# A decayed linear attention feeding a three-way maxout layer: a new order of all engines' instructions

## The chip, the cores and the metric

The kernel runs on one core of one Trainium2 chip. The metric is the device time of one execution in microseconds (us), lower is better; three executions of the kernel before gave 149.94, 150.0 and 150.5 us.

## The reference

Two parts, one after the other. The first is a gated linear attention over 4 batches, 8 heads, 768 tokens and 48 channels a head; the second is a layer over all 3072 tokens with three weight matrices, of whose products the largest is kept.

```
for t in range(S):                                   # S = 768
    state = alpha[:, :, t, :, None] * state + einsum('bhd,bhe->bhde', k[:, :, t], v[:, :, t])
    y[:, :, t] = einsum('bhd,bhde->bhe', q[:, :, t], state)
x = y.transpose(0, 2, 1, 3).reshape(3072, 384)
h = maximum(maximum(x @ w1, x @ w2), x @ w3)         # 384 -> 768
out = h @ w_out                                      # 768 -> 384
```

All inputs and the output are float32 in the chip's main memory.

## The kernel before, in words

**Steps.** The recurrence is done in chunks. The tokens are cut into 12 steps s, each of 256 tokens of one batch: batch s % 4, chunk of tokens s // 4. Within a step the work splits into two units x = 0, 1 of 128 tokens. Inside a unit the products of all pairs of tokens are formed at once (scores, mask, values); between units the state, 48 x 48 a head, is carried on. The layer then runs over the 256 tokens of the step: nine products into PSUM (three blocks jg of 256 columns of the hidden layer, three weights g) and, last, the output product for each unit.

**Pieces.** All work is cut into pieces, and a text called ORDER lists them; `emit` walks through that list and issues each piece's instructions on its engine. A piece is written as a letter, an index, sometimes an engine's letter, and the step: `q1v@3` is piece q with index 1 of step 3 on VectorE. The engine letters are v (VectorE, DVE in the profile), p (GpSimd, POOL) and a (ScalarE, ACT). The engine letter on a load chooses the queue that issues it: SyncE's (SP) without a letter, ScalarE's with a. Without another choice each engine runs its pieces strictly in the order in which the list has them, and waits at a piece until what that piece reads is there and what it writes is free.

The letters, with the function and the line that the profile shows:

| letter | function | engine | what it does |
|---|---|---|---|
| l0, l1, l2, l3 | load_step (L96) | SP or ACT queue | loads alpha (tile ra), k (rk), q (rq), v (rv) of a step, 384 KB each |
| K, W | load_weight (L107, L110), cast_weight | queue; POOL or ACT | one of 12 pieces of 384 KB of the weights into tile ws, then its cast into wcat or wo |
| H | warm (L435) | PE | so many 512-column products of zeros, whose result nobody reads |
| m, N, r | pair_decay, logs, inverse (L183, L187, L192, L194) | DVE/POOL, ACT | product of two tokens' decays, logarithms, the inverse of a decay |
| c | sums (L207, L209) | PE | running sums of the logarithms (tile lps) |
| f, e, g | decay_out, decay_in, totals (L221, L217, L225) | ACT | exponentials of those sums (tiles ac, ic, ge) |
| u, w | near_k, near_q (L198, L202) | DVE/POOL | k and q of every first token times its neighbour's decay (tiles ka, qa) |
| k, q | scale_k, scale_q (L231) | DVE/POOL | k and q times the exponentials (tile qk) |
| V, v | values, unit_values (L155, L157; copies L149, L151) | any | v in 16 bits (tile vt), then in the layout of a unit (tile vu) |
| T, t | turn, keep_turned (L265; copies) | PE; DVE/ACT | transposes of qk through PSUM, and the copy out (tile qkT); steps 0 to 4 |
| D | turn_by_dma (L273) | SP queue | the same by a transposing DMA; steps 5 to 11 |
| A, a | scores, masked (L286, L293) | PE, DVE | products of all pairs (two PSUM tiles aps), masked on the way out (tile lat) |
| Y, x | attend (L306), keep_x | PE; DVE/ACT | the attention's output (tile yps), copied out as the layer's input xT |
| S, s, M, z, y | update (L357), add_state (L367), gates (L344), decay_state (L372), spread_state | PE, DVE, POOL, ACT | the state: product, sum, gate factors, decay, copy in 16 bits (tile st) |
| G, h | gate (L388), maxed (L405; copies) | PE; ACT, DVE | a product of the layer (tile gps; index 3 jg + g), and its maximum with the one before |
| O, o | project (L421), store (L155, L157; DMA L430) | PE; ACT/DVE, SP | the output product (tile ops), scaled out (tile ob) and stored |

A copy or a multiplication through a helper is seen in the profile at the helper's line: L149 and L151 for copies, L155 and L157 for multiplications by a column.

**What ties the pieces.** Loads go into rings of four tiles for each of alpha, k, q and v, so the load of step s waits until the pieces of step s - 4 have read their tile. PSUM has eight banks, taken in turn by every product on PE; scores take two at a time. Weights come in as float32 into eight staging tiles. Output tiles, transposed tiles and the others have two to eight buffers. The order of the list is written out; nothing in the kernel computes it.

Of the kernel before, what the change touches and what calls it, by code (L numbers as in the profile page):

```python
# [23 lines left out]
def kernel(  # L24
# [422 lines left out]
    def emit(order):  # L447
# [14 lines left out]
        g0@3 K5@0 K3@0 e0@3 h1v@0 V0a@2 S0@2 s0a@2 h0v@1 q0p@2 h1v@1 T0@2 t0a@2 t1v@2 W5p@0 G5@1
        G5@0 W3a@0 z0p@2 y0a@2 s1v@2 l0@4 v1p@2 h2v@0 K4@0 h2v@1 r0@4 A1@2 A0@2 a0@2 G3@1 h3a@1
        Y3@2 m0p@4 W4p@0 l3a@3 a3@2 G3@0 N0@4 a1@2 v0p@2 l1@3 r0@3 G4@1 c0@4 g0@4 a2@2 Y2@2
        x1v@2 h3a@0 Y0@2 x0a@2 u0p@3 h4v@1 l0@5 G4@0 h5v@1 M1p@0 z1p@0 y1a@0 G0@2 h0a@2 G5@2
        r1@3 G1@2 K6@0 W6a@0 G3@2 h4v@0 h5v@0 h1v@2 G2@2 l2@3 k0p@3 w0v@3 q0v@3 K7@0 G6@2 V0a@3
        h3a@2 l2@4 l1@4 r1@4 m0p@5 M0p@3 h2v@2 G4@2 h4v@2 k1p@3 S0@3 s0v@3 N0@5 G6@1 h6a@2 h5v@2
        W7p@0 r0@5 G7@2 h7v@2 T0@3 q1p@3 T1@3 G7@1 z0p@3 K8@0 e0@4 w0p@4 f0@4 l3@4 s1v@3 v0a@3
        t1v@3 t0a@3 k1v@4 G6@0 h6a@1 q1p@4 h7v@1 l2@6 u0p@4 c0@5 A0@3 a0@3 A1@3 T1@4 q0p@4 a2@3
        W8a@0 G8@2 a3@3 h8v@2 G8@0 g0@5 h6a@0 a1@3 f0@5 G8@1 k0p@4 T0@4 e0@5 h8v@1 G7@0 v1p@3  # L470
        Y0@3 Y2@3 t1a@4 V0a@4 t0a@4 h7v@0 y0p@3 Y3@3 x0a@3 x1a@3 K11@0 l1@5 K9a@0 v1p@4 S0@4
        W11a@0 A0@4 s0v@4 K10a@0 a1@4 A1@4 a3@4 M0p@4 z0p@4 s1v@4 u0p@5 G0@3 l0@6 a0@4 G7@3
        l1a@6 a2@4 v0v@4 y0a@4 m0p@6 r0@6 G3@3 h3a@3 G1@3 G6@3 Y0@4 r1@5 l3a@5 h0v@3 Y3@4 h8v@0
        Y2@4 x1v@4 N0@6 Y1@4 x0a@4 W9a@0 l2@5 G8@3 M1v@1 c0@6 e0@6 f0@6 G0@4 h1v@3 k0v@5 q1v@5
        G3@4 w0v@5 q0v@5 M0p@5 W10a@0 g0@6 u0v@6 r1@6 G1@4 l0@7 m0v@7 G2@4 k1p@5 D1@5 h0a@4
        z1p@1 k0p@6 O0@1 h1v@4 w0v@6 D0@5 q0p@6 D0@6 k1p@6 q1p@6 O1@1 N0@7 l0@8 h6a@3 l3@6 h2v@4
        l2@7 l1a@7 o1a@1 h7v@3 D1@6 h3v@4 o0a@1 V0a@5 O0@2 o0a@2 O1@2 y1p@1 G7@4 h8v@3 S0@5 A0@5
        s0v@5 o1a@2 a0@5 a1@5 A1@5 a3@5 a2@5 v1a@5 z0p@5 G4@4 v0p@5 r0@7 u0p@7 y0a@5 G2@3 G6@4
        s1v@5 M1p@2 z1p@2 y1p@2 h4v@4 c0@7 Y3@5 Y1@5 Y2@5 m0p@8 Y0@5 e0@7 k0p@7 h2v@3 h6v@4
        h7v@4 G5@4 x0a@5 f0@7 G4@3 x1a@5 l1@8 N0@8 G8@4 V0a@6 h8v@4 r1@7 w0p@7 G0@5 h0a@5 h5v@4  # L480
        h4v@3 k1v@7 G3@5 h3a@5 G1@5 h1v@5 c0@8 e0@8 g0@7 f0@8 M1p@3 G5@3 h5v@3 G4@5 Y1@6 A1@6
        g0@8 M0p@8 r0@8 h4v@5 A0@6 a1@6 l3@7 S0@6 s0v@6 M0p@6 q0v@7 D0@7 q1p@7 z0p@6 D1@7 G6@5
        a3@6 h6a@5 G7@5 l0@9 l2@8 G5@5 G2@5 z1p@3 O0@0 s1v@6 v1a@6 a2@6 y0a@6 y1p@3 v0a@6 Y3@6
        a0@6 Y2@6 Y0@6 O1@0 x1v@6 o0a@0 l0@10 r1@8 l3a@8 x0v@6 G4@6 G3@6 V0a@7 v1a@7 G0@6 h5v@5
        M1v@4 z1p@4 G8@5 h2v@5 h3a@6 h7v@5 h4v@6 S0@7 h0a@6 v0p@7 l3@11 o1a@0 h8v@5 y1a@4 A0@7
        a1@7 s0v@7 u0p@8 A1@7 a2@7 m0p@9 a3@7 M0p@7 z0p@7 y0p@7 k0p@8 Y1@7 a0@7 r0@9 l1a@9 G2@6
        G1@6 h1v@6 q1p@8 G6@6 h6v@6 s1v@7 G5@6 Y0@7 Y2@7 N0@9 l2@9 m0v@10 w0v@8 q0p@8 D0@8 Y3@7
        k1v@8 D1@8 x0a@7 x1a@7 l3@9 G8@6 G7@6 r1@9 G6@7 h6a@7 G0@7 V0v@8 c0@9 e0@9 O1@3 g0@9
        M1p@5 u0v@9 k0v@9 O0@3 f0@9 w0p@9 G4@7 q1p@9 k1p@9 D1@9 q0p@9 D0@9 o1a@3 o0a@3 V0a@11
        h2v@6 h5v@6 h7v@6 h8v@6 G8@7 G7@7 h7v@7 h0a@7 S0@8 N0@10 s0v@8 O0@5 o0a@5 A0@8 a0@8 A1@8  # L490
        a2@8 l0@11 Y1@8 G3@7 v1a@8 h3a@7 l1a@10 O1@5 c0@10 a3@8 z0p@8 y0p@8 Y3@8 o1a@5 a1@8 Y2@8
        e0@10 h8v@7 g0@10 v0p@8 Y0@8 G1@7 x0a@8 f0@10 V0a@9 v0p@9 x1v@8 G1@8 h4v@7 l2@10 M1v@6
        z1v@6 z1v@5 y1a@5 l3@10 G0@8 h1v@7 M0p@9 h0a@8 S0@9 A1@9 A0@9 s0v@9 z0p@9 y0p@9 G6@8
        l1@11 G2@8 a0@9 v1p@9 G2@7 G5@7 h6a@8 r0@10 r1@10 M0p@10 u0p@10 Y3@9 a3@9 a1@9 a2@9
        m0v@11 l2a@11 q1p@10 k1v@10 D1@10 Y0@9 Y1@9 x0a@9 Y2@9 G7@8 h2v@7 h1v@8 x1a@9 r0@11 G4@8
        G8@8 G6@9 G3@9 w0p@10 N0@11 c0@11 f0@11 h5v@7 e0@11 h6v@9 V0v@10 q0v@10 k0p@10 D0@10
        O0@4 O1@4 g0@11 v0a@10 h7v@8 h2v@8 G4@9 h8v@8 G5@8 O1@7 r1@11 v1p@10 S0@10 h3a@9 h4v@9
        o0a@4 o1a@4 q1p@11 k1v@11 o1a@7 M1p@7 D1@11 s0v@10 A0@10 a0@10 A1@10 a3@10 u0p@11 k0p@11
        G7@9 z0p@10 y0a@10 y1p@6 G8@9 G3@8 h3a@8 O0@7 a1@10 w0v@11 a2@10 h7v@9 h8v@9 Y3@10 Y1@10
        Y0@10 Y2@10 G1@9 G0@9 x1v@10 x0a@10 G4@10 z1p@7 q0p@11 D0@11 h4v@8 h0a@9 h5v@8 h1v@9  # L500
        G2@9 G3@10 o0a@7 v1p@11 h2v@9 S0@11 s0v@11 A0@11 A1@11 a0@11 a3@11 h3a@10 G6@10 G0@10
# [42 lines left out]
```

## Time and profile before

| what | value |
|---|---|
| time, median of 3 runs (lowest to highest) | 150.0 us (149.94 to 150.5) |
| span of the profiled execution, first to last instruction | 147.1 us |
| time of the profiled execution itself | not on the page; the median is 2.9 us above its span |
| PE busy | 137.7 us, 94% of the span |
| DVE, ACT, POOL busy | 120.5, 100.7, 89.7 us |
| DMA | 32.43 MB, 220 GB/s on average |
| TensorE clock granted | 1.000 |

Busy times of a line of the profile are the union of its instructions; an instruction's duration is a mean over its group. An "idle before" time says how long the engine stood before the instruction, and the name behind the arrow is what ended the wait. A row of the timeline has the start, the time taken, the engine (with a q behind it where only the engine's sequencer works, as in issuing a DMA), the line, the operation and the tiles, out before in.

### The profile page before, as it was taken

The numbers are of one execution on the slowest core, as the hardware profiler recorded it, in microseconds if no ns is written. First come the engines' busy times: TensorE is split into PE (matmuls) and PEld (weight loads), VectorE is DVE, ScalarE is ACT, GpSimd is POOL, SyncE is SP. The second block draws the span as 40 slices with busy tenths as digits, with TensorE's granted clock in tenths as the row PEclk, the third lists the DMA queues.
The fourth block names the chain that finished last, engine by engine and source line by source line (L and its number), as shares of the span: only waits on it lengthen the run. The fifth ranks groups of instructions, "written<-read, shape, count | busy, mean of one in ns | idle before, by whom it ended". The sixth has DMA issues, their size and how long they took to land.

```text
span 147.1 us, 5524 instructions
## 1 busy us (share of the span) xinstructions
PE 137.7 (94%) x2301; PEld 105.4 (72%) x2301; DVE 120.5 (82%) x224; ACT 100.7 (68%) x207; POOL 89.7 (61%) x147
## 2 busy tenths in 40 slices
...
GB/s 114 321 325 341 326 312 282 322 288 334 328 298 241 286 225 155 202 289 187 303 156 325 327 218 155 237 269 276 288 117 222 91 113 0 4 75 37 53 241 134
DMA packets 73032, 32.43 MB, mean 220 GB/s; under 512 B 65456, under 2 KB 73008, under 8 KB 73008
## 3 DMA queue, kind: packets, MB, share of 16 engines
...
q10 hardware_dynamic: 9152, 4.03, 10.5%
...
## 4 chain that ended last, share of the span: by engine, by line
PE 38%; DMA 18%; POOL 16%; ACT 9%; SPq 8%; issue 4%; DVE 4%; POOLq 0%; DVEq 0%; ACTq 0%
PE gps L388 21%; DMA rv<-in_v_dram 11%; PE ops L421 10%; SPq L96 7%; POOL qk L231 6%; DMA ws<-in_moe_w_dram 5%; PE yps L306 3%; DMA qkT<-qk 3%; POOL kept L372 2%; POOL ka L198 2%; PE aps L286 2%; POOL st L151 2%; ACT vu L149 1%; POOL wcat L151 1%; POOL vu L151 1%
## 5 line engine op out<-in xcount | busy, mean ns | idle before, releaser
L388 PE MATMUL gps<-xT,wcat 128*128 128x256 f16 x648 | 76.5, 273 | 1.5 <-DVE hT L405 0.6
L388 PEld LDWEIGHTS <-wcat 128*128 128x128 f16 x648 | 61.2, 98 | 11.7 <-issue 1.1
L293 DVE TENSOR_TENSOR lat<-aps,cp 128x512 f16<-128x512 f32 x48 | 30.3, 681 | 0.5 <-PE aps L286 0.3
L405 DVE TENSOR_TENSOR h<-gps,h 128x512 f16<-128x512 f32 x36 | 24.6, 684 | 2.4 <-PE gps L388 1.2
L405 DVE TENSOR_TENSOR hT<-gps,h 128x512 f16<-128x512 f32 x36 | 24.1, 684 | 1.9 <-PE ops L421 1.3
L421 PE MATMUL ops<-wo,hT 128*128 128x384 f16 (+1 forms) x150 | 25.2, 320 | 0.2 <-ACT h L149 0.2
L149 ACT CAST h<-gps 128x512 f16<-128x512 f32 x28 | 16.2, 583 | 9.0 <-PE gps L388 7.0
L421 PEld LDWEIGHTS <-hT 128*128 128x128 f16 x150 | 14.1, 98 | 8.2 <-issue 0.4
L155 ACT ACTIVATE ob<-ops,c 128x384 f32<-128x384 f32 (+1 forms) x23 | 12.2, 567 | 11.4 <-PE ops L421 11.3
L372 POOL TENSOR_TENSOR kept<-full,gm 128x192 f32<-128x192 f32 x18 | 10.3, 573 | 10.5 <-DVE gm L344 5.0
L151 POOL COPY vu<-vt 64x384 f16<-64x384 f16 x24 | 12.2, 509 | 4.7 <-ACT vt L155 2.8
L149 ACT CAST xT<-yps 128x384 f16<-128x384 f32 x17 | 7.8, 490 | 7.3 <-PE yps L306 7.3
L231 POOL TENSOR_TENSOR qk<-ka,ic 128x384 f16<-128x384 f32 x10 | 10.5, 1054 | 3.6 <-ACT h L149 2.6
L149 ACT COPY vu<-vt 64x384 f16<-64x384 f16 x22 | 11.2, 510 | 0.7 <-DVE vt L157 0.3
L435 PE MATMUL wps<-wo 128*128 128x512 f16 x35 | 9.7, 425 | 1.2 <-DVE wo L511 1.2
L155 ACT ACTIVATE vt<-rv,c 128x768 f16<-128x768 f32 x10 | 9.4, 941 | 1.6 <-DMA rv<-in_v_dram 1.5
L231 POOL TENSOR_TENSOR qk<-rq,ac 128x384 f16<-128x384 f32 x8 | 8.3, 1036 | 1.7 <-DMA rq<-in_q_dram 1.7
L286 PE MATMUL aps<-qkT 48*64 48x128 f16 x384 | 7.7, 219 | 1.3 <-DVE qkT L151 0.8
L198 POOL TENSOR_TENSOR ka<-rk,ra 128x384 f32<-128x384 f32 x8 | 8.4, 1044 | 0.2
L306 PE MATMUL yps<-lat,vu 128*32 128x128 f16 x384 | 8.0, 220 | 0.3 <-DVE lat L293 0.2
L231 POOL TENSOR_TENSOR qk<-rk,ic 128x384 f16<-128x384 f32 x6 | 6.2, 1040 | 3.1 <-DMA rk<-in_k_dram 3.0
L192 ACT ACTIVATE ra<-ra 128x384 f32<-128x384 f32 x12 | 6.3, 524 | 2.5 <-DMA ra<-in_alpha_dram 2.4
...
## 6 DMA issues: line engine op xcount, KB each, us to landing
...
```

Source lines behind the costliest of these rows:

```text
L149: nc.scalar.copy(out=dst, in_=src)
L151: engines[eng].tensor_copy(out=dst, in_=src)
L155: nc.scalar.mul(dst, src, col)
L198: engines[eng or "p"].tensor_mul(near_of[s, "k"], raw("k", s, 0), raw("a", s, 1))
L231: engines[eng or "p"].tensor_mul(dst.rearrange("p a b c -> p (a b) c")[:, :, :D], near_of.pop((s, n)) if r == 0 else raw(n, s, r), dec_of[ ...
L286: nc.tensor.matmul(aps[i][r * J:(r + 1) * J, a * U + x, :], qkT[rows, r, 1, p, cols], qkT[rows, :, 0, p, cols], start=True, stop=True)
L293: nc.vector.tensor_mul(lat_of[s, u][:, i], aps_of[s, u][i], pmask.unsqueeze(1).broadcast_to([P, HP, P]))
L306: nc.tensor.matmul(y_of[s, x][C * m:C * (m + 1), f, :], lhs, rhs, start=(s, x, m) not in begun, stop=last[x] and n == len(todo) - 1)
L372: engines[eng or "p"].tensor_mul(kept, full_of.pop((s, x)), gm_of.pop((s, x)).unsqueeze(2).broadcast_to([P, HP, D]))
L388: nc.tensor.matmul(gps[:, j, :], wcat[:, f, g, jj * P:(jj + 1) * P], xT[:, f].rearrange("p u t -> p (u t)"), start=(f == 0), stop=(f == NF ...
L405: nc.vector.tensor_max(h, gps, h_of[s, i - 1])
L421: nc.tensor.matmul(ops_of[s, o], hT_of[s][:, jj, u * P:(u + 1) * P], wo16[:, jj, cols], start=(jj == 0), stop=(jj == NJ - 1))
```

## The change

The list ORDER is replaced by another. Both have the same 818 pieces: no piece, tile or buffer is added or taken away. What differs is the order, on every engine, and the engine or queue of some pieces:

| pieces | engine or queue before | after |
|---|---|---|
| loads l | SP 40, ACT 8 | SP 29, ACT 19 |
| weight loads K | SP 10, ACT 2 | SP 7, ACT 5 |
| weight casts W | ACT 8, POOL 4 | ACT 5, POOL 7 |
| values V | ACT 10, DVE 2 | ACT 7, DVE 2, POOL 3 |
| unit_values v | ACT 11, POOL 12, DVE 1 | ACT 15, POOL 9 |
| scale_q q | POOL 14, DVE 10 | POOL 10, DVE 14 |
| scale_k k | POOL 16, DVE 8 | POOL 17, DVE 7 |
| near_q w | DVE 7, POOL 5 | DVE 4, POOL 8 |
| near_k u, pair_decay m | DVE 4 and 6, POOL 8 and 6 | DVE 5 and 7, POOL 7 and 5 |
| gates M | POOL 17, DVE 3 | POOL 13, DVE 7 |
| decay_state z | POOL 18, DVE 2 | POOL 13, DVE 7 |
| spread_state y | POOL 10, ACT 9, DVE 1 | POOL 9, ACT 11 |
| keep_x x | ACT 17, DVE 7 | ACT 14, DVE 10 |
| store's scaling o | ACT 23, DVE 2 | ACT 17, DVE 8 |
| maxed h, add_state s | one h from ACT to DVE | one s from DVE to ACT |

The start and the end of both lists:

```diff
     ORDER = """
-        l0@0 r0@0 H12@0 H4@0 H1@0 m0p@0 N0@0 c0@0 r1@0 l0@1 m0v@1 l2@0 H1@0 r0@1 f0@0 g0@0 H4@0
-        w0p@0 l1@0 u0v@0 q0v@0 N0@1 c0@1 e0@0 l3@0 V0a@0 r1@1 e0@1 f0@1 l0@2 k1v@0 q1v@0 M0p@0
-        l2@1 k0p@0 l1@1 k1p@1 m0v@2 w0v@1 H10@0 g0@1 N0@2 S0@0 s0a@0 T1@0 t1a@0 c0@2 q1v@1 T0@0
-        z0p@0 f0@2 e0@2 g0@2 q0v@1 H1@0 l3@1 V0a@1 t0v@0 A1@0 A0@0 T1@1 H2@0 u0v@1 a2@0 k0p@1
-        S0@1 T0@1 K1@0 v1a@0 v0p@0 a1@0 a3@0 a0@0 Y0@0 W1a@0 Y2@0 t1v@1 y0p@0 s0a@1 M0p@1 z0p@1
-        Y3@0 l0@3 v1a@1 t0v@1 m0v@3 A1@1 A0@1 x0a@0 x1a@0 G1@0 K2@0 W2p@0 G2@0 l1@2 a2@1 v0a@1
-        y0p@1 Y3@1 k1p@2 u0p@2 a1@1 N0@3 c0@3 a3@1 a0@1 Y0@1 r0@2 r1@2 K0@0 W0a@0 x0v@1 Y2@1
-        x1a@1 l2@2 s1v@0 s1v@1 f0@3 k0p@2 w0v@2 G0@0 l3@2 M0p@2 G1@1 G0@1 G2@1 h0a@0 q1v@2 T1@2
...
-        G6@11 h6a@11 G4@11 O1@9 h4v@11 O0@9 o0v@9 h2v@11 O0@6 O1@10 o1a@10 O1@6 h7v@11 h5v@11
-        O4@11 h8v@11 o1a@9 O6@11 o0a@6 o1a@6 o2a@11 O2@11 O3@11 o0a@11 O5@11 o1a@11 O0@10 o0a@10
+        H12@0 H10@0 l0@0 m0v@0 r0@0 H4@0 l0@1 N0@0 m0v@1 r1@0 c0@0 H1@0 r0@1 l2@0 f0@0 g0@0 q1v@0 w0v@0
+        N0@1 r1@1 l1a@1 H1@0 H2@0 e0@0 l1@0 l0a@2 c0@1 l3a@1 g0@1 M0p@0 u0v@0 M0v@1 k1v@0 k0v@0 T1@0 l1a@2
+        q0v@0 T0@0 f0@1 t1v@0 l3@0 l2@1 q1v@1 V0a@0 e0@1 v1a@0 w0p@1 u0v@1 S0@0 H4@0 K1a@0 k1v@1 t0a@0
+        m0v@2 K0a@0 A1@0 s0a@0 z0p@0 A0@0 r0@2 r1@2 k0p@1 l2a@2 a2@0 a1@0 T1@1 N0@2 V0a@1 H1@0 K2@0 v0a@1
+        c0@2 S0@1 l3a@2 a0@0 q0v@1 s0a@1 e0@2 v0p@0 y0p@0 W1a@0 T0@1 z0p@1 y0p@1 a3@0 t1v@1 Y0@0 Y2@0
+        t0v@1 Y3@0 x0v@0 K4@0 A1@1 x1a@0 A0@1 a2@1 a1@1 G1@0 W0a@0 l0@3 G0@0 g0@2 a0@1 a3@1 W2p@0 G2@0
+        f0@2 v1a@1 Y3@1 h0a@0 q1v@2 w0v@2 Y0@1 u0v@2 x0a@1 M0p@2 Y2@1 x1a@1 k1p@2 T1@2 h1v@0 k0v@2 G1@1
+        q0p@2 G0@1 T0@2 t1a@2 W4a@0 h2v@0 h0a@1 G4@1 s1v@1 s1v@0 V0p@2 t0a@2 S0@2 A1@2 h1v@1 v1a@2 v0p@2
+        m0v@3 a3@2 A0@2 G4@0 N0@3 a0@2 s0a@2 K3@0 W3p@0 G2@1 z0p@2 l0@5 m0p@5 K5@0 W5p@0 c0@3 K6a@0 r0@3
...
+        Y1@9 Y2@9 Y0@9 G4@8 x0a@9 O1@7 x1v@9 h4v@8 D0@11 h2v@8 h5v@8 G0@9 h0a@9 G1@9 S0@10 V0v@11 A0@10
+        o1a@7 A1@10 v1a@11 a0@10 a3@10 h1v@9 O0@8 s0v@10 a1@10 G6@9 h6a@9 a2@10 O1@8 S0@11 A0@11 s0v@11
+        o0a@8 A1@11 G7@9 M0p@10 z0p@10 a1@11 a2@11 y0p@10 y1a@6 G3@9 a0@11 v0p@11 z0v@11 G4@9 G2@9 G5@9
...
+        h4v@11 o0a@9 h5v@11 O2@11 h8v@11 O3@11 o0v@10 o1a@10 o0v@11 O4@11 O5@11 O6@11 o1a@11 o2v@11
     """
```

SP's queue up to l3@4 has, in the old order: l0@0 l0@1 l2@0 l1@0 l3@0 l0@2 l2@1 l1@1 l3@1 K1 l0@3 K2 l1@2 K0 l2@2 l3@2 K5 K3 l0@4 K4 l1@3 l0@5 K6 l2@3 K7 l2@4 l1@4 K8 l3@4; in the new order: l0@0 l0@1 l2@0 l1@0 l3@0 l2@1 K2 K4 l0@3 K3 l0@5 K5 l0@4 l2@3 l1@3 l1@4 l3@3 K7 K8 l2@4 l3@4. ACT's queue has, in the old order: l3@3 K9 K10 l1@6 l3@5 l1@7 l3@8 l1@9 l1@10 l2@11; in the new order: l1@1 l0@2 l3@1 l1@2 K1 K0 l2@2 l3@2 K6 l0@6 K11 K10 l2@5 l3@5 l0@7 l2@6 l3@6 l0@10 l0@11 l2@9 l1@9 l1@11 l2@11 l2@10.

More of the change, by code (lines that the diff above doesn't have):

```diff
@@ L460 @@
-        y0p@1 Y3@1 k1p@2 u0p@2 a1@1 N0@3 c0@3 a3@1 a0@1 Y0@1 r0@2 r1@2 K0@0 W0a@0 x0v@1 Y2@1
-        x1a@1 l2@2 s1v@0 s1v@1 f0@3 k0p@2 w0v@2 G0@0 l3@2 M0p@2 G1@1 G0@1 G2@1 h0a@0 q1v@2 T1@2
[L462 to L501, printed above, removed]
@@ L502 @@
-        M0p@11 z0p@11 G5@9 G1@10 y0v@11 a1@11 y1a@7 Y1@11 Y3@11 v0a@11 a2@11 Y0@11 Y2@11 h4v@10
-        G2@10 x0a@11 G8@10 x1a@11 G8@11 G5@10 h5v@9 G5@11 h6a@10 h0v@10 h1v@10 G0@11 h0v@11 O0@8
-        o0v@8 O1@8 o1a@8 h5v@10 G7@10 G3@11 h7v@10 h3a@11 G1@11 h8v@10 h2v@10 G2@11 h1v@11 G7@11
-        G6@11 h6a@11 G4@11 O1@9 h4v@11 O0@9 o0v@9 h2v@11 O0@6 O1@10 o1a@10 O1@6 h7v@11 h5v@11
-        O4@11 h8v@11 o1a@9 O6@11 o0a@6 o1a@6 o2a@11 O2@11 O3@11 o0a@11 O5@11 o1a@11 O0@10 o0a@10
+        H12@0 H10@0 l0@0 m0v@0 r0@0 H4@0 l0@1 N0@0 m0v@1 r1@0 c0@0 H1@0 r0@1 l2@0 f0@0 g0@0 q1v@0 w0v@0
@@ new lines @@
+        f0@2 v1a@1 Y3@1 h0a@0 q1v@2 w0v@2 Y0@1 u0v@2 x0a@1 M0p@2 Y2@1 x1a@1 k1p@2 T1@2 h1v@0 k0v@2 G1@1
+        q0p@2 G0@1 T0@2 t1a@2 W4a@0 h2v@0 h0a@1 G4@1 s1v@1 s1v@0 V0p@2 t0a@2 S0@2 A1@2 h1v@1 v1a@2 v0p@2
+        m0v@3 a3@2 A0@2 G4@0 N0@3 a0@2 s0a@2 K3@0 W3p@0 G2@1 z0p@2 l0@5 m0p@5 K5@0 W5p@0 c0@3 K6a@0 r0@3
+        a2@2 r1@3 G3@1 a1@2 s1v@2 h2v@1 G3@0 Y0@2 y0a@2 N0@5 g0@3 h3v@0 Y3@2 x0v@2 h3a@1 h4v@0 h4v@1 l0@4
+        Y2@2 x1a@2 f0@3 c0@5 G5@1 e0@3 l2@3 q1v@3 m0p@4 G3@2 w0p@3 M0v@3 l1@3 k1v@3 N0@4 e0@5 h3a@2 G0@2
@@ new lines @@
+        G5@0 c0@4 u0v@3 h0a@2 f0@4 q0v@3 T1@3 G1@2 r0@4 h5v@0 g0@4 G2@2 h5v@1 k0p@3 T0@3 r1@4 l1@4 l3@3
+        t1v@3 g0@5 G4@2 e0@4 h1v@2 G5@2 h4v@2 f0@5 W6p@0 K7@0 G6@0 K8@0 l0a@6 u0p@4 h2v@2 t0a@3 V0a@3
+        h5v@2 A0@3 M0p@4 a1@3 k0p@4 S0@3 l2@4 w0v@4 K11a@0 A1@3 M0p@5 G6@2 W7a@0 s0a@3 G7@2 W8p@0 a3@3
+        K10a@0 a0@3 h6a@0 v0a@3 z0p@3 s1v@3 l3@4 h6a@2 y0a@3 K9@0 h7v@2 r0@5 q1p@4 l2a@5 q0p@4 G8@2 l1@5
+        G6@1 h6a@1 G7@0 V0a@4 a2@3 G8@0 l1@7 k1p@4 T0@4 T1@4 t1a@4 G7@1 M1v@0 v1p@3 h8v@2 h7v@0 t0v@4 Y0@3
@@ new lines @@
+        x0a@3 l3a@5 Y2@3 Y3@3 h8v@0 x1v@3 A1@4 W10a@0 A0@4 a2@4 S0@4 m0p@6 G1@3 z1p@0 G0@3 W9p@0 l0@8
+        h7v@1 l1@6 W11p@0 r1@5 s0v@4 O1@2 r0@6 w0p@5 u0v@5 o1a@2 O0@2 l0a@7 a0@4 N0@6 r1@6 G8@1 k1p@5 a1@4
+        l2a@6 c0@6 f0@6 l2@7 q0v@5 h0v@3 q1p@5 D1@5 G2@3 h8v@1 O0@0 z0p@4 y0p@4 g0@6 a3@4 M1p@2 k0v@5 D0@5
+        h1v@3 m0v@8 l1@8 y1a@0 l3a@6 h2v@3 s1v@4 v0a@4 O1@1 O0@1 G6@3 v1a@4 Y2@4 z1v@2 o0a@1 Y3@4 N0@8
+        M1p@1 V0p@5 e0@6 h6v@3 o0a@0 z1p@1 M0p@6 Y0@4 x1a@4 Y1@4 S0@5 c0@8 e0@8 o0a@2 m0v@7 G7@3 x0v@4
@@ new lines @@
+        g0@8 s0v@5 G0@4 h0a@4 k1p@6 G1@4 f0@8 h7v@3 o1a@1 G8@3 G2@4 N0@7 z0v@5 G3@4 s1v@5 h1v@4 q1v@6
+        h8v@3 V0a@6 h3a@4 c0@7 h2v@4 u0p@6 M1v@4 e0@7 k0p@6 y1p@2 w0p@6 q0v@6 G6@4 h6a@4 g0@7 v1a@6 A0@5
+        D1@6 S0@6 a1@5 s0v@6 r0@8 A1@5 a3@5 D0@6 y1a@1 G7@4 G3@3 l0@9 G8@4 h7v@4 l3@7 G4@3 a2@5 h8v@4
+        v1p@5 r0@7 a0@5 G5@3 h3a@3 h4v@3 u0p@8 z0p@6 l0a@10 v0a@5 M0p@7 r1@7 h5v@3 y0p@5 O1@0 Y3@5 s1v@6
+        l2@8 Y1@5 Y0@5 Y2@5 k1p@8 A0@6 x0v@5 a1@6 x1a@5 A1@6 O0@3 f0@7 l3@8 u0p@7 w0p@7 G4@5 m0p@9 a0@6
@@ new lines @@
+        G0@5 k0p@7 l0a@11 k1p@7 o1a@0 N0@9 q0v@7 a3@6 D0@7 q1p@7 V0v@7 G1@5 l2a@9 h0a@5 h1v@5 c0@9 G3@5
+        m0v@10 v1p@7 e0@9 h3a@5 D1@7 N0@10 G5@5 G6@5 h4v@5 h5v@5 q1p@8 h6a@5 g0@9 M1p@3 o0a@3 a2@6 G7@5
+        h7v@5 M1p@5 D1@8 l1a@9 G8@5 h8v@5 G2@5 h2v@5 v0a@7 f0@9 l3@9 G4@4 z1v@4 M0p@8 r1@8 z1p@5 c0@10
+        G5@4 h4v@4 O0@5 y0p@6 O1@5 h5v@4 r0@9 w0p@8 Y3@6 q0p@8 v0a@6 o1a@5 z1v@3 o0v@5 Y0@6 r0@10 k0p@8
+        Y1@6 x0v@6 D0@8 Y2@6 S0@7 x1a@6 u0p@9 A0@7 y1a@3 r1@10 a1@7 q1p@9 g0@10 A1@7 G3@6 a2@7 a3@7 s0v@7
@@ new lines @@
+        G0@6 G4@6 a0@7 G1@6 h3a@6 h0v@6 M1v@6 k0v@9 z0p@7 G5@6 s1v@7 m0p@11 O1@4 h4v@6 V0a@8 v1a@8 l1a@11
+        y0a@7 G6@6 h5v@6 o1a@4 l2a@11 h6a@6 G2@6 O1@3 V0p@9 h1v@6 h2v@6 k1p@9 S0@9 o1a@3 A1@8 D1@9 N0@11
+        A0@8 S0@8 a2@8 s0v@9 Y3@7 e0@10 r1@9 Y2@7 x1a@7 v0p@8 z1p@6 a3@8 Y0@7 Y1@7 x0a@7 G7@6 l2a@10 h7v@6
+        c0@11 G8@7 G6@7 s0v@8 l1@10 G0@7 a0@8 f0@11 w0v@9 G8@6 a1@8 G7@7 h8v@6 q0v@9 D0@9 g0@11 v0p@9 G1@7
+        e0@11 M0p@9 O1@6 G4@7 h0a@7 h1v@7 h6a@7 q1v@11 O0@6 h7v@7 l3@10 o0v@6 u0p@11 M1v@7 y1a@4 f0@10
```

8 lines of the change are left out of this document (added).

## The prediction

> **What bounds the kernel now.** First the page's busy shares, then the busy times by stretch.
>
> ```profile
> PE 137.7 (94%) x2301; PEld 105.4 (72%) x2301; DVE 120.5 (82%) x224; ACT 100.7 (68%) x207; POOL 89.7 (61%) x147
> ```
>
> ```profile
> 0.00:5.00 5.00, 3.81 (x12) 1.53 (x13) 2.62 (x19) 1.81 (x2) 4.41 (x16) 1.00 0.68 166
> 5.00:10.00 5.00, 4.83 (x31) 2.25 (x29) 2.37 (x4) 3.37 (x8) 2.73 (x4) 1.00 1.17 325
> 10.00:15.00 5.00, 3.67 (x96) 2.53 (x95) 4.59 (x9) 4.88 (x12) 2.02 (x4) 1.00 1.15 336
> 15.00:20.00 5.00, 4.01 (x129) 2.70 (x126) 4.95 (x10) 4.84 (x11) 4.60 (x9) 1.00 1.10 329
> 25.00:30.00 5.00, 5.00 (x117) 4.01 (x116) 4.83 (x10) 3.90 (x8) 4.33 (x7) 1.00 1.07 307
> 120.00:130.00 10.00, 9.94 (x174) 8.24 (x174) 7.04 (x14) 3.55 (x8) 0.51 (x1) 1.00 0.07 21
> ```
>
> After the colon pair come the stretch's length and the busy time of PE, PEld, DVE, ACT and POOL, then the granted clock, the DMA share and GB/s. From 25 us on PE is full. Before that ACT and DVE are nearly full from 10 us, and the DMA engines are full from 5 us at about 330 GB/s, 1.2 us for a 384 KB load.
>
> PE's least work comes from unbroken runs in the chain of waits, such as this one:
>
> ```profile
> 130.72 4.58 PE gps L388 x42
> ```
>
> That is 0.109 us a matmul, 70.7 us for 648. In the same way ops is 23.4 (1.95 for 12), yps 10.0 (0.90 for 56), aps 5.5 (0.46 for 32), tps 4.5 (0.45 for 8), sps 3.7 (0.37 for 32), lps 2.9 (0.24 for 5): 120.7 us, the same in both orders. The span is 147.1. The other 26.4 us are: the start, 15.5 (G0@0, from which PE runs on without a break, starts at 22.5 with 7.0 us of that work done); the end, 4.0 (the last matmul ends at 143.1); and 6.9 in between. Of the 6.9, I count real stops of 0.75 at G8@8, 0.37 at A0@3, 0.36 at O1@7, 0.27, 0.25 and 0.21 and a few smaller, about 2.9; the rest is some 0.1 us at a change from one kind of matmul to another. There are 109 such changes in the old order and 112 in the new, so this does not move. A new order can win only at the start, in the 2.9 us, and at the end.
>
> **How the start goes now.** The timeline of the first 13 us:
>
> ```profile
> 0.74 1.08 SPq L96 DMA_DIRECT2D ra<-in_alpha_dram  x2
> 1.87 1.33 SPq L96 DMA_DIRECT2D rq<-in_q_dram  x1
> 3.24 1.20 SPq L96 DMA_DIRECT2D rk<-in_k_dram  x1
> 4.42 0.52 ACT L192 ACTIVATE ra<-ra 128x384 f32<-128x384 f32 x1 [2.41 <-DMA ra<-in_alpha_dram]
> 6.18 0.33 PE L207 MATMUL lps<-la,cp 128*128 128x384 f16 x1
> 6.75 0.47 ACT L221 ACTIVATE ac<-lps 128x384 f32<-128x384 f32 x1
> 7.04 1.00 POOL L202 TENSOR_TENSOR qa<-rq,ra 128x384 f32<-128x384 f32 x1 [1.58 <-DMA rq<-in_q_dram]
> 8.19 0.56 DVE L198 TENSOR_TENSOR ka<-rk,ra 128x384 f32<-128x384 f32 x1 [1.91 <-DMA rk<-in_k_dram]
> 13.05 1.12 POOL L231 TENSOR_TENSOR qk<-rk,ic 128x384 f16<-128x384 f32 x1 [2.98 <-DMA rk<-in_k_dram]
> ```
>
> Loads leave SP in order and arrive 1.2 us apart: first at 4.4, q0 at 7.0, k0 at 8.2, k1, the eighth, at 13.0. The third and later issues take 1.2 us or more, the time of a transfer: once some two loads are waiting, the issuer is held until room comes free.
>
> **The change at the start, step by step.**
>
> *Warming matmuls.* All 35 stay, but 26 instead of 17 now stand ahead of c0@0. Old: six at 0.43 us, then 0.215 each. 1.2 + 6 x 0.43 + 20 x 0.215 = 8.1, so c0@0 goes from 6.2 to 8.1 and f0@0, ACT's first user of it, from 6.75 to 8.6.
>
> *Loads on ACT's queue.* k1, a2, v1, k2, K1, K0, q2 and v2 move from SP to ACT, between its activations. SP runs on with q1, K2, K4, a3, K3, which nobody needs so early (q1 apart), until l0@5 waits for u0v@1, which needs k1. What an issue costs ACT, when there is room, is seen here:
>
> ```profile
> 29.11 0.53 ACT L192 ACTIVATE ra<-ra 128x384 f32<-128x384 f32 x1
> 29.40 0.42 ACTq L96 DMA_DIRECT2D rv<-in_v_dram  x1
> 29.54 0.57 ACT L149 CAST h<-gps 128x512 f16<-128x512 f32 x1
> 30.01 0.52 ACT L187 ACTIVATE la<-pa 128x384 f16<-128x384 f32 x1
> ```
>
> Nothing: the sequencer issues under a running activation. But k1, a2 and v1 come within 1 us, at about 9.5, 10.0 and 10.5, and k2 behind g0@1. By the SP rows the third is held until the first has gone through. Alone that is at about 12.5; with SP's backlog of four loads beside it, 13 to 14.5. Behind the held l3a@1 stand g0@1 (and on DVE M0v@1, then k1v, k0v, q0v@0 behind that), and behind the held l1a@2 stand f0@1, V0a@0 and all of ACT. I take 13.1 for g0@1 and 15.6 for f0@1; with no hold they would be 10.9 and 11.4.
>
> *ACT from there to G0@0.* From f0@1 to W0a@0 the durations of the rows, less 0.1 each where two overlap, are: five activations of 0.42 or less (f0, e0 twice, N0, and x1a@0) 1.9; r0, r1@2 0.85; V0a twice 1.7; v1a@0 and v0a@1 2.1; t0a@0 0.9; s0a twice 0.55; W1a, W0a 1.5: 9.5 us. From 15.6 that is 25.1, so G0@0 at about 25.3, with 5.5 us of PE work done (c0@3, Y3, Y0, Y2@1 and G2@0 now come after it). The loss is 19.8 against 15.5. Bounds: with no hold, from 11.4, 20.9 by ACT alone, but K0 is then the 16th load, 4.4 + 15 x 1.2 = 22.4 plus a 0.8 cast, 23.2, loss 17.7; if the two queues share evenly, ACT's loads land every 2.4 us from 14.4, K0 at 26.4, G0@0 at 27.3, loss 21.8. The nearest row is an ACT load under SP traffic, the one above, issued at 29.40 and landed 6.5 us later, the same as SP's neighbours: between the two, so I stay at 19.8. The Trainium skill ("DMA: Bandwidth & Descriptors", Issuing engines are not separate DMA queues) says that transfers from several issuers run on the same 16 engines and interleave, and that a second issuer saves only issue time; it speaks against this move, and the 6.5 us agrees.
>
> *Does it come back soon?* From W0a to x1a@2, ahead of G3@2, ACT has another 10.6 us (of them v1a twice 2.1, t1a and t0a@2 1.8): 35.7, where PE has 15.4 of its work done, loss 20.3. Until there ACT, not PE, sets the pace. After that its queue is lighter than PE's. Old loss at the same work: 16.2. So +4.1.
>
> PE also stands idle for about 4 us between c0@1 and T1@0 at the new start; the longest gap there now is 1.2. The Trainium skill ("TensorE: Matmul & The Clock Gate", What's actually happening) halves the clock after some 3.4 us idle; by it the sum would be up to 1.3 us higher, but no run so far shows it, and I leave it out.
>
> **The rest of the change.** *Engines.* DVE gains 6 ob x 0.62, 5 kept x 0.36, 3 xT x 0.56, 4 gm x 0.16, 4 qk x 0.6 and three single ones of 0.6 to 0.7, and loses 3 qa x 0.76 and four small ones: +7.6, to 128. ACT loses 5 (to 96). POOL gets three vt products that no row shows: between the 128x768 cast, 0.82, and twice the 384-wide product, 2.1; it ends at 85 to 89. All stay below the 147, so I cost this at nothing, under PE's runs of G. If DVE's cover fails it is where the new order has A0, A1@10 and A0, A1@11 close together: 9.3 us of DVE work in 8 of PE's. *Late loads.* l3@10 stood behind four stores on SP and took 9.45 us; it and its neighbours are now asked for earlier, on ACT or ahead of the stores. I give back 1.0 of the 2.9 us of stops, bounds 2.9 and -1.5 (as many new ones). *End.* The last product is now a half (0.17) and its copy and store are halves: 0.58 to 0.43 and 1.85 to 1.74, -0.25.
>
> **Sum.** +4.1 - 1.0 - 0.25 = +2.85, span 150.0. The page gives no time of its own beside the span; the runs' median, 150.0, is 2.9 above it, and I keep that: **152.9**.
>
> **Rivals.** *Faster, 149.0:* ACT is never held and loads land in order of issue. G0@0 at 23.2 costs +2.2, all 2.9 us of stops go, the end gives 0.25: -0.95. It decides if l1a@2 is issued before 12 and W0a is done by 23.3. For: issues in the rows cost ACT nothing. Against: no row has three 384-byte-row loads in a burst on ACT, and SP's burst was held. *Even sharing, 155.5:* SP's early weights and a5, K5, a4 halve the rate of ACT's urgent loads, G0@0 at 27.3, +6.3, less 0.75 for stops and end. *DVE as a second bound, 154.5:* the main case, with 1.5 us of new stops at s = 8 to 11. *No change, 150.0:* the start costs +3.2 (loss 18.7) and nearly all the stops go.
>
> **Chances.** Main case 0.50 (own range 151 to 154.5), even sharing 0.18, DVE 0.10, no change 0.09, faster 0.13. Differences under 0.5%, 0.75 us, can't be told from none here. So slower 0.78, same 0.09, faster 0.13. The range 150.0 to 156.5 leaves out the faster case and the far end of even sharing.
>
> **What would show it.** Right: c0@0 near 8.1; ACT's third and fourth load issues longer than 1 us; G0@0 between 24.5 and 26.5; PE full from about 36 us; stops after that under 2 us. Wrong: G0@0 at or before 23.2, or ACT's issues all at 0.4 us, or stops of several us after 40 us.

## The result and the profile after

The changed kernel takes 159.9 us (median; 159.0 to 162.4) against 150.0: 1.066 of the time before, 95% interval 1.058 to 1.073. Forecast were 152.9 and a range up to 156.5: the direction was right, the size less than a third (2.9 us against 9.9). The profiled execution took 160.5 us with a span of 158.4, 11.3 above the old one.

The busy shares and the stretches of the changed kernel, columns as before:

```profile
PE 141.7 (89%) x2301; PEld 108.5 (69%) x2301; DVE 127.9 (81%) x240; ACT 97.7 (62%) x204; POOL 90.2 (57%) x134
```

```profile
5.00:10.00 5.00, 5.00 (x27) 2.30 (x26) 0.71 (x2) 1.98 (x6) 0.00 (x0) 1.00 1.17 327
10.00:15.00 5.00, 1.01 (x14) 0.60 (x12) 2.23 (x6) 1.47 (x5) 1.72 (x2) 1.00 1.14 346
15.00:20.00 5.00, 4.46 (x86) 2.56 (x84) 3.61 (x8) 4.88 (x9) 0.86 (x2) 0.66 1.14 338
25.00:30.00 5.00, 3.54 (x30) 2.52 (x30) 3.75 (x7) 4.49 (x10) 3.17 (x7) 0.59 1.17 322
30.00:35.00 5.00, 4.80 (x78) 3.79 (x76) 2.71 (x6) 3.05 (x6) 4.68 (x5) 0.73 0.88 239
```

From 10 to 15 us ACT is busy for 1.5 us where it was busy for 4.9, and PE for 1.0 instead of 3.7, while the DMA engines stay as full as they were. So the loads kept moving, but the engines waited for others than those that came. The granted clock (the third number from the end) falls below one in three stretches: it is halved from 15.7 to 19.1 and from 25.9 to 32.8 us, in the old kernel at no time between 3.9 us and the end.

For each kernel below I give one more number: how far PE is behind when it has done 15 us of its work, with the least time of each piece as the measure (a layer product of 6 matmuls 0.655, an output product 0.975, and so on). It is the start of that piece minus the work done before it. Before: 16.2 us; changed: 26.7, so 10.5 of the 11.3 us are lost by then. From there until 119 us of work are done, the old kernel loses 6.8 more and the changed one 8.0. The last matmul ends 4.0 us before the end of the span in the old kernel, 3.5 in the new. Each number is from one trace, and one trace can be off by a microsecond or so: seven traces that have the same 17 warming products ahead of c0@0 start it between 6.2 and 7.5 us (the last section says why).

The ACT engine and its queue in the timeline of the changed kernel:

```profile
9.33 0.49 ACT L221 ACTIVATE ac<-lps 128x384 f32<-128x384 f32 x1 [3.02 <-PE lps L209]
9.34 0.42 ACTq L96 DMA_DIRECT2D rk<-in_k_dram  x1
9.83 0.63 ACTq L96 DMA_DIRECT2D ra<-in_alpha_dram  x1
10.49 3.27 ACTq L96 DMA_DIRECT2D rv<-in_v_dram  x1
13.81 0.27 ACT L225 ACTIVATE ge<-lps,c 128x16 f32<-128x16 f32 x1 [2.62 <-issue]
13.83 1.11 ACTq L96 DMA_DIRECT2D rk<-in_k_dram  x1
14.99 0.49 ACT L221 ACTIVATE ac<-lps 128x384 f32<-128x384 f32 x1 [0.91 <-issue]
24.60 0.38 ACTq L96 DMA_DIRECT2D rv<-in_v_dram  x1
25.02 0.32 ACT L149 COPY full<-sps 128x192 f32<-128x192 f32 x1 [2.60 <-DMA ra<-in_alpha_dram]
```

The issue of the third load, v1, lasts 3.27 us, and the activation behind it, g0@1, starts when it is over; the fourth, k2, holds f0@1. Later ACT stands 2.60 us before it issues v2. That issue needs no data. The release is the landing of alpha of step 5, a load of SP's queue, at 24.58: the trace shows eight signals of completion, shared by the loads of both queues in turn, and a load that is to use one waits for the load that used it last. The same is seen at K3 on SP (issued at 15.15, k1 landed at 15.14), K1 (16.36, a2 at 16.34) and K0 (17.56, v1 at 17.54).

PE in the same trace:

```profile
14.80 0.40 PE L265 MATMUL tps<-cp,qk 128*128 128x128 f16 x4 [3.71 <-DVE qk L231]
17.27 1.89 PE L435 MATMUL wps<-wo 128*128 128x512 f16 x4
26.88 4.00 PE L388 MATMUL gps<-xT,wcat 128*128 128x256 f16 x18 [1.08 <-ACT xT L149]
```

T1@0 waits 3.71 us for DVE, which waits for g0@1. After it the four warming products take 0.43 us apart again, and three layer products after 26.88 take 4.0 us where 2.0 would do. The Trainium skill ("TensorE: Matmul & The Clock Gate", What's actually happening) says the clock is halved after some 3.4 us idle; behind this wait the trace agrees, with a clock of 0.66 from 15 to 20 us. But so long a wait is not needed: before the clock fell at 25.9 us PE had not stood for more than 0.85 us in one piece since the wait that ended at 14.8, and in the run with the early loads on SP, below, it fell at 13.7 us after a longest wait of 1.66.

After 40 us, PE's waits, the four longest of the changed kernel and then all of the old one:

```profile
PE aps L286 <- DMA qkT<-qk: 0.7, 1, 0.7
PE gps L388 <- DVE lat L293: 0.7, 1, 0.7
PE ops L421 <- DVE hT L405: 0.6, 1, 0.6
PE sps L357 <- DVE lat L293: 0.6, 1, 0.6
```

```profile
PE gps L388 <- DVE hT L405: 0.6, 1, 0.6
PE aps L286 <- ACT qkT L149: 0.2, 1, 0.2
PE ops L421 <- ACT h L149: 0.2, 1, 0.2
```

### The profile page after: what moved, and what is told of

It reads as the page before. It is cut to its first block, busy times and chain, and to the rows that moved or that the text cites. A ratio compares the mean times of both kernels' runs of the same rounds, so it can differ in the third digit from the quotient of the medians.

```text
span 158.4 us, 5517 instructions
## 1 busy us (share of the span) xinstructions
PE 141.7 (89%) x2301; PEld 108.5 (69%) x2301; DVE 127.9 (81%) x240; ACT 97.7 (62%) x204; POOL 90.2 (57%) x134
## 3 DMA queue, kind: packets, MB, share of 16 engines
q10 hardware_dynamic: 21792, 9.54, 23.7%
## 4 chain that ended last, share of the span: by engine, by line
PE 33%; POOL 6%; DMA 5%; issue 2%; DVE 2%; ACT 2%; SPq 1%; POOLq 0%; DVEq 0%; ACTq 0%
PE gps L388 20%; PE ops L421 8%; DMA rv<-in_v_dram 5%; PE yps L306 3%; POOL qk L231 3%; POOL vt L157 2%; PE aps L286 1%; PE sps L357 1%; DVE h L405 1%; DVE lat L293 1%; POOL qa L202 1%; ACT h L149 1%; POOL pa L183 1%; POOL ka L198 1%; ACT vu L149 1%
## 5 line engine op out<-in xcount | busy, mean ns | idle before, releaser
L388 PE MATMUL gps<-xT,wcat 128*128 128x256 f16 x648 | 78.9, 277 | 2.4 <-ACT xT L149 1.1
L149 ACT CAST h<-gps 128x512 f16<-128x512 f32 x27 | 15.6, 587 | 20.7 <-PE gps L388 12.6
L405 DVE TENSOR_TENSOR hT<-gps,h 128x512 f16<-128x512 f32 x36 | 24.1, 683 | 1.3 <-PE gps L388 0.4
L372 POOL TENSOR_TENSOR kept<-full,gm 128x192 f32<-128x192 f32 x13 | 7.0, 535 | 25.6 <-DVE full L367 12.8
L421 PEld LDWEIGHTS <-hT 128*128 128x128 f16 x150 | 14.3, 98 | 8.3 <-DVE hT L405 0.9
L155 ACT ACTIVATE ob<-ops,c 128x384 f32<-128x384 f32 (+1 forms) x17 | 9.7, 572 | 10.4 <-PE ops L421 10.3
L149 ACT COPY vu<-vt 64x384 f16<-64x384 f16 x30 | 15.3, 509 | 0.4
L265 PE MATMUL tps<-cp,qk 128*128 128x128 f16 x80 | 6.9, 235 | 4.5 <-DVE qk L231 4.5
L151 POOL COPY vu<-vt 64x384 f16<-64x384 f16 x18 | 9.7, 538 | 1.3 <-DVE vt L157 0.6
L231 POOL TENSOR_TENSOR qk<-rk,ic 128x384 f16<-128x384 f32 x9 | 9.9, 1102 | 0.8 <-ACT ic L217 0.7
L202 POOL TENSOR_TENSOR qa<-rq,ra 128x384 f32<-128x384 f32 x8 | 8.5, 1068 | 2.6 <-ACT ra L194 2.4
L286 PEld LDWEIGHTS <-qkT 48*64 48x64 f16 x384 | 6.5, 106 | 4.6 <-issue 2.3
L221 ACT ACTIVATE ac<-lps 128x384 f32<-128x384 f32 x12 | 5.9, 495 | 5.1 <-PE lps L209 4.2
```

What stands on the lines that cost most here:

```text
L149: nc.scalar.copy(out=dst, in_=src)
L151: engines[eng].tensor_copy(out=dst, in_=src)
L155: nc.scalar.mul(dst, src, col)
L202: engines[eng or "p"].tensor_mul(near_of[s, "q"], raw("q", s, 0), inv1_of.pop(s))
L231: engines[eng or "p"].tensor_mul(dst.rearrange("p a b c -> p (a b) c")[:, :, :D], near_of.pop((s, n)) if r == 0 else raw(n, s, r), dec_of[ ...
L286: nc.tensor.matmul(aps[i][r * J:(r + 1) * J, a * U + x, :], qkT[rows, r, 1, p, cols], qkT[rows, :, 0, p, cols], start=True, stop=True)
```

## The experiments

Theory A: the start is nearly the whole loss, and in it the loads on ACT's queue, in two ways: they hold ACT, and they arrive late. The rivals are the late c0@0 behind 26 warming products with the clock (B), the new order of the other pieces at the start (C), and the new rest. Ratios are to the kernel before on the same chip. "Lost" is the number explained above, by 15 us of work, and from 15 to 119.

| kernel | median us | ratio, 95% interval | lost by 15 | lost 15 to 119 |
|---|---|---|---|---|
| before | 150.0 | 1 | 16.2 | 6.8 |
| changed | 159.9 | 1.066, 1.058 to 1.073 | 26.7 | 8.0 |
| old start, new rest, first splice | 157.8 | 1.050, 1.041 to 1.059 | 24.6 | 7.7 |
| new start, old rest | 160.5 | 1.070, 1.062 to 1.078 | 26.8 | 8.0 |
| changed, early loads on SP | 153.6 | 1.022, 1.013 to 1.031 | 20.7 | 8.1 |
| changed, warming as before | 159.6 | 1.066, 1.057 to 1.074 | 25.9 | 7.6 |
| changed, early loads on SP and warming as before | 152.4 | 1.020, 1.013 to 1.027 | 18.7 | 7.8 |
| changed, SP alone, loads in the changed order of arrival | 157.1 | 1.054, 1.045 to 1.063 | 23.6 | 7.6 |
| changed, 30 more warming products | 158.4 | 1.059, 1.049 to 1.068 | | |
| changed, v2 on SP | 158.0 | 1.058, 1.051 to 1.065 | 24.0 | 8.0 |
| old start, new rest, second splice | 153.3 | 1.028, 1.019 to 1.038 | 19.2 | 7.4 |
| before, with the eight loads on ACT | 159.4 | 1.068, 1.058 to 1.077 | 25.9 | 6.1 |
| before, 26 warming products first | 151.5 | 1.016, 0.999 to 1.033 | 17.5 | 7.0 |
| before, late loads re-ordered | 149.6 | 1.001, 0.997 to 1.005 | 16.3 | 6.4 |

**Old start, new rest.** Two lists spliced: the list is the old one up to Y2@1, then all that is left in the new order.

> The old order up to and with Y2@1 (the last attention product before the layer runs without a break), then every remaining piece in the new order. Theory A, the start is nearly the whole loss: the changed kernel lost 26.5 us by G3@1 against 16.1 before, and only 1.2 us more than the old one after that, so about 151. Rival, the new rest (a heavier DVE, other load order) costs by itself: 154 or more. If the splice lets the rest run without the late start, its own stops show after 40 us.

157.8 us, as the rival said, but not for its reason: G0@0 starts at 22.4 as in the old kernel, and then PE stands for 6.2 us, so that T1@2 starts at 29.4 and not at 25.2. In the old list the load of q of step 2 stands right behind the cut; after the splice it leaves by ACT with SP's run of later loads beside it, and lands at 28.7 and not at 22.4. The cut made a new late load. It was done again further on:

> The old order up to and with T1@2, which takes in the loads of q and v of step 2 that the first splice left late, then the rest in the new order. Theory A: PE runs on as in the old kernel from 22.5 us, and the new rest adds its own 1 to 1.5 us: 150.5 to 152. Rival: the new rest is worse by itself than the two traces side by side say (7.0 against 8.2 us lost after 12 us of work): 154 or more.

153.3 us. PE has lost 15.5 us by 10 us of work, as before, and then stops twice: 1.39 us before G4@1, behind ACT's cast of weights that the two orders place differently, and 0.93 us inside A0@2, behind ACT's s0a@2. From 15 us of work on it loses 7.4, 0.6 us more than the old kernel, which is within what single traces differ by. Two splices can't tell more, since each joint makes stops of its own.

**New start, old rest.**

> The mirror: the new order up to and with Y2@1, then every remaining piece in the old order. Theory A: about 158 to 160, as slow as the changed kernel. Rival, the rest is at fault: 154 or less.

160.5 us, as theory A has it. The new start is enough for the whole loss. Behind it the old rest loses 8.0 us, as much as the new rest does, so the 1.2 us that the changed kernel loses more than the old one after the start are not shown to be the new rest's.

**The early loads back on SP.** The engine letters and the order of the first loads, all else as in the new list:

```diff
-  l0@1 ... l2@0 ... l1a@1 ... l1@0 l0a@2 l3a@1 ... l1a@2 ... l3@0 l2@1 ... K1a@0 ... K0a@0 ... l2a@2 ... K2@0 ... l3a@2 ... l0@3
+  l0@1 l2@0 l1@0 l3@0 l0@2 l2@1 l1@1 l3@1 K1@0 l0@3 K2@0 l1@2 K0@0 l2@2 l3@2
```

> The new order with the early loads (steps 0 to 2, K0, K1, K2 and l0@3) back on SP in the old order's sequence; all else as in the new order, the 26 warming products ahead of c0@0 too. Theory A, loads on ACT's queue hold ACT (3.3 and 1.1 us in the issue, 2.6 us waiting for another load to land) and come late (K1 at 21.0, K0 at 24.9): with them gone the start keeps only the 2.7 us later c0@0; G0@0 near 24 and no half clock after 25 us, time 153 to 155. Rival B, the late c0@0 and the clock are the cause: no better than 158.

153.6 us, G0@0 at 24.1, inside what theory A gave. ACT's timeline no longer has the holds:

```profile
11.39 0.49 ACT L217 ACTIVATE ic<-lps 128x384 f32<-128x384 f32 x1
11.76 0.28 ACT L225 ACTIVATE ge<-lps,c 128x16 f32<-128x16 f32 x1
11.92 0.51 ACT L221 ACTIVATE ac<-lps 128x384 f32<-128x384 f32 x1
22.71 0.85 ACT L149 CAST wcat<-ws 128x768 f16<-128x768 f32 x1
```

g0@1 starts at 11.76 and not at 13.81, and W0a@0, the last row, at 22.71 and not at 26.70, though c0@0 came later here (9.6 against 8.9). The loads make 6.0 of the 10.5 us.

**The mirror: those eight loads moved, in the old kernel.** On SP, K2 and alpha of step 3 trade places with it, and no other piece moves.

```diff
-  l0@2 ... l1@1 ... l3@1 ... K1@0 l0@3 K2@0 l1@2 K0@0 ... l2@2 l3@2            (all SP)
+  N0@1 l1a@1 ... e0@0 l0a@2 l3a@1 ... r1@1 l1a@2 ... l2@1 K2@0 l0@3 ... t1a@0 K1a@0 ... g0@2 K0a@0 ... V0a@1 l2a@2 ... v1a@1 l3a@2
```

> The old order with one part of the new: k1, a2, v1, k2, K1, K0, q2 and v2 issued by ACT between its activations, SP running on with q1, K2, a3 and what follows. Warming products and all else as before. Theory A: the third and fourth of the burst hold ACT for 3 to 6 us together, and K1 and K0 land near 21 and 24: 153 to 157. Rival: the old start has room on ACT (c0@0 at 6.2) and takes it up: 150 to 151.5.

159.4 us: this one part by itself, in the old order, costs as much as the whole change, and more than I expected. Its rows show both ways of costing:

```profile
9.09 2.45 ACTq L96 DMA_DIRECT2D rv<-in_v_dram  x1
11.59 0.93 ACT L155 ACTIVATE vt<-rv,c 128x768 f16<-128x768 f32 x1 [2.22 <-issue]
13.87 0.38 ACTq L96 DMA_DIRECT2D rk<-in_k_dram  x1
14.29 0.49 ACT L217 ACTIVATE ic<-lps 128x384 f32<-128x384 f32 x1 [1.35 <-DMA rk<-in_k_dram]
17.52 0.56 DVE L183 TENSOR_TENSOR pa<-ra 128x384 f32<-128x384 f32 x1 [6.29 <-DMA ra<-in_alpha_dram]
25.86 0.83 ACT L149 CAST wcat<-ws 128x768 f16<-128x768 f32 x1 [3.29 <-DMA ws<-in_moe_w_dram]
```

ACT is held 2.2 us in the issue of v1 and 1.35 before that of k2, which waits for k1 to land; DVE waits 6.29 us for alpha of step 2, which lands at 17.5 and not at 10.5, and ACT 3.29 us for K1. By 15 us of work 9.7 us more are lost than in the old kernel, and not 6.0 as above. Up to 1.3 of them are a later c0@0 (7.5), which no edit made. For the rest I only have an argument: the old order has little to do until alpha of step 2 is there, and the new one places it later.

**Held or late?** The loads all on SP, in the sequence in which they landed in the changed kernel:

```diff
+  (SP) l0@0 l0@1 l2@0 l1@0 l3@0 l2@1 K2 K4 l0@3 l1@1 l0@2 l3@1 l1@2 K3 K1 ... l0@5 K0 K5 l2@2 l0@4 l2@3 l3@2
```

> The new order with the early loads issued by SP alone, but in the sequence in which they landed in the changed kernel's trace (q1, K2, K4, a3 ahead of k1, a2, v1, k2, then K3, K1, a5, K0, K5, q2, a4, q3, v2). It keeps the late arrival and takes away what holds ACT. If ACT being held is the cost: 154 to 156. If the late arrival of k1, a2, v1, K1, K0, q2 and v2 is the cost, whoever issues them: 158 or more. No change of the 26 warming products.

157.1 us, between the two. By 15 us of work 23.6 us are lost: 3.1 less than in the changed kernel, 2.9 more than with the old sequence. That would make about half of the loads' 6.0 us ACT held and half the late arrival. The ratios put it otherwise: from 1.066 to 1.054, with intervals that overlap, without the hold, and from 1.054 to 1.022 with the early arrival as well. So the late arrival's cost is shown, at about half or more; the hold's share lies between nothing and about half. The landings are not quite those of the changed kernel either: K1 comes 1.6 us later, q2 and v2 1.0 and 0.7 earlier. The halved clock goes along and is in these shares: after 25 us it lasts 6.8 us in the changed kernel, 3.4 here, and none with the old sequence. ACT's largest waits from 5 to 30 us of this kernel are, in total, 3.3 us for alpha, 3.0 for PE's sums and 2.9 for weights; none is in an issue.

**One load, v2, on SP.**

> The changed kernel with one load, v of step 2, on SP and not on ACT (it goes between K2 and K4). ACT stood 2.6 us before that issue, until alpha of step 5 had landed on SP's queue at 24.58. If this wait delays s0a@1, W1a, x1a@0 and so G1@0: G1@0 at 24.5 and not 26.9, and with a shorter idle time before it perhaps no half clock: 155 to 158. If K1 and K0, which land at 21.0 and 24.9 or later with one load more ahead of them, are what G waits for: 159 to 160.

158.0 us, with an interval that overlaps the changed kernel's; G1@0 at 25.4. The 2.6 us wait before s0a@1 is gone: it starts at 22.78 and not at 25.02. W1a@0 then waits for its weights, which land at 24.1. Of the 2.7 us less lost, 0.7 are an earlier c0@0, which no edit made (see below).

**The warming products.** Back in their old places, in the changed kernel and, beside the early loads on SP, in the kernel that has them there:

```diff
-  H12@0 H10@0 ... H4@0 ... c0@0 H1@0 ... H1@0 H2@0 ... c0@1 ... S0@0 H4@0 ... T1@1 ... H1@0
+  H12@0 H4@0 H1@0 ... c0@0 H1@0 H4@0 ... c0@1 H10@0 ... S0@0 H1@0 ... T1@1 H2@0
```

> The new order with the 35 warming products back where the old order has them relative to c0@0, c0@1, S0@0 and T1@1 (17 ahead of c0@0, 10 behind c0@1); loads as in the new order. Theory A: c0@0 goes from 8.9 to about 6.3, ACT's burst of loads is issued some 2 us earlier but is held just as long or longer, since SP's backlog is the same: 157 to 159. Rival B: the start is gained back with c0@0 and PE stays warm through the wait for T1@0: 154 to 155.

> The new order with both changes of the two runs before at once: early loads on SP in the old sequence, and the warming products in their old places. Theory A (loads first, then the late c0@0): the start is all but the old one, loss near 17 to 18 us when 15 us of PE's work is done (16.2 before, 20.7 with the loads alone, 26.7 changed), time 150.5 to 152. Rival C, the new order of the other pieces at the start costs too: stays at 153 to 154.

159.6 and 152.4 us. By themselves they win nothing: c0@0 is earlier (7.4), but the issues of v1 and k2 are held again (2.5 and 2.2 us), K1 lands at 22.9, v2 still waits for alpha of step 5 to land (25.2), and G1@0 starts at 27.5, no earlier than in the changed kernel. With the loads on SP, 2.0 us less are lost by 15 us of work, but of the 3.4 us by which c0@0 comes earlier (6.2, not 9.6) some 1.5 are a shorter slow phase of PE in that trace (see the last section); the two ratios, 1.022 and 1.020, don't tell the kernels apart. What stays, 2.5 us above the old start, is left, by elimination, to the new order of the other pieces there (rival C): c0@2, for one, starts at 16.5 where the old kernel has 12.0, and the new list has r0@2 and r1@2 ahead of N0@2 on ACT; no run tried that pair alone. The reverse in the old kernel:

> The old order with the warming products placed as in the new: 26 ahead of c0@0. c0@0 and f0@0 come some 2 us later. If ACT is the pace of the old start from 9.3 us on, the delay is partly taken up in its waits for loads before that: 151 to 152. If the loads' arrival is the pace: 150.

151.5 us, 1.3 us more lost: of the 2.2 us that c0@0 comes later, a part is taken up. The interval touches 1.

**More warming in PE's waits.**

> The changed kernel with 30 more warming products in PE's waits (18 behind c0@1, 4 behind Y3@0, 8 behind A0@1), to keep the clock up. The trace showed a granted clock of 0.66 from 15 to 20 us and 0.59 and 0.73 from 25 to 35. If the clock costs by itself, G1@0 to G0@1 run at 0.66 us each and not at 1.25, and 2 to 3.5 us are won: 156.5 to 158. If ACT and the loads set the pace there whatever PE's clock: 159 to 161, PE waiting where it was slow before.

158.4 us with an interval that overlaps the changed kernel's; its profiled execution took 162.5 us, too far from that to be read beside the others. The clock's own price isn't settled by this: the 30 products fill the waits, but also stand in front of what comes next. A sign that it has one is in the run with v2 on SP, where the granted clock is 1.00 from 25 us on: from G1@0 to G2@1 it takes 10.1 us, in the changed kernel 11.3. That was only read, not tried apart. A bound: the clock is halved for 10.2 us in the changed kernel, so at most 5.1 us can be its price.

**A faster old kernel?** The trace of before shows two late loads, at DVE; v of step 11 was loaded 20 us before it was needed.

```diff
-  ... l3@11 ... l0@11 ... l3@10 ...        V0a@11 behind o0a@3
+  ... l0@11 ... l3@10 ... l3@11 ...        V0a@11 behind o1a@7
```

> The old order with three late loads re-ordered on SP: alpha of step 11 and v of step 10 trade places with v of step 11, so that they no longer stand behind four stores (v of step 10 took 9.45 us; DVE waited 1.41 and 0.89 us for the two); V0@11 moves behind o1a@7. If these waits made PE's stops at G8@8 (0.75) and O1@7 (0.36): 148.9 to 149.3, faster than both kernels. If the stops only move on to the stores or to v of step 11: 150.

149.6 us, ratio 1.001: no difference. The stops at G8@8 and O1@7 are gone, and PE waits elsewhere instead:

```profile
111.48 0.64 PE L286 MATMUL aps<-qkT 48*64 48x128 f16 x32 [0.39 <-DMA qkT<-qk]
120.22 0.64 PE L286 MATMUL aps<-qkT 48*64 48x128 f16 x32 [0.41 <-DMA qkT<-qk]
```

The scores of steps 10 and 11 now wait for their transposing DMAs, which they did not in the old kernel. No run here beats the kernel before.

## Why the prediction was right or wrong, step by step

- *What bounds it, and where an order can matter:* right. 10.5 of 11.3 us are lost before 15 us of PE's work is done.
- *Warming products, c0@0 at 8.1:* it came at 8.9. The slow phase of PE lasted 10 products and not 6, which is chance and worth 0.9 us.
- *ACT held at the third load:* right, and well sized: g0@1 at 13.8 (13.1 forecast), f0@1 at 15.0 (15.6).
- *ACT from f0@1 to W0a@0, 9.5 us, G0@0 at 25.3:* this is the step that failed first, and the next stretch of ACT, below, failed with it: 20.1 us for the two, 26.9 measured. This one took 12.6, and G0@0 came at 28.1. The sum had ACT's issues cost something only where the queue is full. It left out the 2.6 us before v2, a wait for a load of the other queue.
- *Arrival:* the bounds of 22.4 and 26.4 for K0 held (24.9), but by neither of their models. k1, a2, v1 and k2 came 1.2 us apart, because SP was itself held until k1 had landed; then, with SP running again, K0, q2 and v2 came 3.1 to 3.9 us apart, more than the 2.4 of even sharing. q2 and v2 (28.0 and 31.2; 22.4 and 23.7 before) were not in the sum at all, which stopped at K0.
- *Clock:* left out, "no run so far shows it". It should have been a term: the forecast itself had the 4 us wait, and the changed kernel ran at half clock behind it and again from 25.9 us. Its price stays open, at most 5.1 us. (The gap of 1.2 us given for the old start is that of the weight loads; PE's own longest wait after 2 us is 0.85.)
- *Until x1a@2, loss 20.3:* x1a@2 ended at 41.8, not 35.7, loss 26.7. The 10.6 us for ACT between was counted as if nothing else held it, and took 14.3; there PE's slow layer products, late q2 and v2 and the 2.35 us product of v on POOL all came in, in shares that no run tells apart.
- *The rest, stops 1.0 us less:* wrong in sign, 1.2 us more, though the old rest loses as much behind the new start. DVE's work was forecast right (128; 127.9), but it was costed at nothing. The waits for DVE listed above come at steps 3 to 8, not at 10 and 11.
- *The end, -0.25:* 4.0 to 3.5 us. *Around the span:* 2.9 forecast, 2.1 in the profiled execution. The recorded executions of the old kernel have about 1.8 between time and span, so the one profiled, with 147.1, took some 148.9: the forecast set a fast execution's span beside the median, and the 11.3 us between the two spans are some 1.4 more than the 9.9 between the medians.

Of the rivals, faster and no change are out: l1a@2 was issued at 13.8, not before 12. Even sharing was the nearest, and too low too, since it kept ACT free of the waits that go with it.
